# Issuing the value products of two attention pieces as one block, ahead of older work

## The chip, the cores and the metric

The kernel runs on one core of a Trainium2 chip. The metric is device time in microseconds. A time is the median of several runs; the profile shows one further execution. The engines are called as in the profile: PE is TensorE (matmuls), PEld its weight loads, DVE is VectorE, ACT is ScalarE, POOL is GpSimd, and SP issues all DMAs, one after the other, each once its own waits are over.

## The reference

Windowed attention with block summaries, then a mixture of experts on its output, all in float32.

```python
def _attn_ref(q, k, v):                      # 4 batches, 8 heads, 768 positions, 64 wide
    block, window = (32, 16)
    k_sum = k.reshape(B, H, nb, block, D).max(axis=3)
    v_sum = v.reshape(B, H, nb, block, D).mean(axis=3)
    scores_l = scale * np.matmul(q, k.transpose(0, 1, 3, 2))
    mask_l = np.abs(pos[:, None] - pos[None, :]) < window
    scores_s = scale * np.einsum('bhsd,bhnd->bhsn', q, k_sum) + np.log(block)
    scores_all = np.concatenate([np.where(mask_l, scores_l, -1e9), scores_s], axis=-1)
    ...                                      # softmax over the last axis -> a
    return np.matmul(a, np.concatenate([v, v_sum], axis=2))

def _moe_ref(x, domain_probs, w1, w2):       # x is (3072, 512); 4 experts, hidden width 1024
    p = domain_probs / (domain_probs.sum(-1, keepdims=True) + 1e-09)
    for e in range(E):
        out += p[:, e:e + 1] * (np.maximum(x @ w1[e], 0.0) @ w2[e])
```

## The kernel before, in words

**Attention.** The work is cut into 64 pieces: piece n is 96 queries of one batch and four of its eight heads; pieces n - 1 and n (n odd) are the two halves of the heads for the same queries. Batch b has pieces 16b to 16b + 15. A piece runs through `load_piece`, `stage_a` (keys ks, queries qs and values v12, v3 split into a high and a low part on ACT and POOL), `scores` (psc on PE, maxima and row sums on DVE and ACT), `probs` (the probabilities aw, in float16 as a high part, a low part and the block summaries), `transposed` (one DMA on SP turns aw into awT), `values` and `to_x`. `values` is 24 matmuls per piece: for two pairs of heads, six terms of two heads each; a matmul has 64 columns of weights and 96 of output, and the two heads write the lower and the upper 64 partitions. Both pieces of a pair write one PSUM bank, called px with the number of the lower piece, so a block is 48 matmuls. `to_x` brings px to the rows of x. The first eight pieces are handled apart, in `first_tokens`.

**Experts.** x is cut into eight token blocks of 384. Products are done in three terms (high x high, low x high, high x low). For blocks 0 and 1, `plain_units` does the first layer (ph, 128x384 outputs) and `mm2` the second (po, 128x512). Blocks 2 to 7 are done in pairs by `pair_units`, with seven first-layer products in place of eight (banks pha, phb, phc, phd; some of them added up on DVE and ACT between the products). High and low parts of weights are made by ACT and POOL (wh and wl), for some on DVE.

**Batches.** For each batch after the first, `setup_k` loads four chunks of k (kch) and reduces each on DVE to ksr, whose spread copy ks goes out with four DMAs; `setup_v` loads four chunks of v (vch), reduces each to vsr, and `stack_v` scales that on ACT (vs5) and turns it on PE with four transposes (pvs). All these chunks, and the rows that `x_operands` reads back, share two buffers (`CHUNKS = 2`).

**What sets the order.** The text of the program issues attention steps between units of the experts: `steps` gives each step a number, and `advance` issues those whose number has come. The first part, up to piece 8, is kept in program order. From there on (`pinned["rest"] = False`) a scheduler arranges the instructions of every engine: it takes, of those that its own estimate of times holds to be ready, the one with the highest priority, which is the order of the text unless a block is given another. Each engine then runs its own list strictly from front to back, so an instruction that waits holds all behind it.

Of the kernel before, what the change touches and what calls it, by code (L numbers as in the profile page):

```python
# [17 lines left out]
B, H, S, D = 4, 8, 768, 64  # L18
# [14 lines left out]
NEG = -1.0e9 / SCALE  # L33

SHIFT = 1.12
ENDS = (17.52, 25.5, 38.0, 53.0, 68.0, 70.0)
WARM = 11

# [24 lines left out]
def attn_moe(ctx: ExitStack, tc: tile.TileContext, qvL, qv0, v0L, kD, kT, vT, w1L, w2L, dpL, cst, out):  # L63
# [18 lines left out]
    V, A, PL, PE = (Engine(e, "rest") for e in (nc.vector, nc.scalar, nc.gpsimd, nc.tensor))  # L82
    SP = Engine(nc.sync, "load")
# [6 lines left out]
    def spare_x(n):  # L90

        return n % 2 == 1 and n < XFREE
# [29 lines left out]
    def aw_of(n):  # L122
        w = spare_x(n)
        if w not in aw_bufs:
            if w:
                t = sb.tile([QB, 3 * G, P], F16, name="aw1", tag="x", bufs=NX)
            else:
                t = const.tile([QB, 3 * G, P], F16, name="aw0")
            PL.memset(t[:, 2 * G : 3 * G, NST:P], 0.0)
            aw_bufs[w] = t  # L130
        return aw_bufs[w]
# [7 lines left out]
    st = {}  # L139
# [156 lines left out]
    def transposed(n):  # L296
        tag, bufs = ("x", NX) if spare_x(n) else ("awT", 2)
        awT = sb.tile([P, 3 * G, QB], F16, name=f"awT{n}", tag=tag, bufs=bufs)
        SP.dma_start_transpose(out=awT, in_=aw_of(n).rearrange("p a k -> p (a k)"))
        st[n]["awT"] = awT  # L300

    def values(n):
        b, g = n // 16, n % 2
        t = st[n]
        awT, (v12, v3), vs = t["awT"], t["v"], vsum[b]
        if g == 0:
            t["bank"] = ps_av.tile([P, 512], F32, name=f"px{n}", tag="av")
        else:
            t["bank"] = st[n - 1]["bank"]
        px = t["px"] = t["bank"][:, g * 2 * QB : (g + 1) * 2 * QB].rearrange("p (c q) -> p c q", q=QB)  # L310
        for c in range(2):
            terms = []
            for j in (2 * c, 2 * c + 1):
                hi, lo, su = awT[:, j, :], awT[:, G + j, :], awT[:NST, 2 * G + j, :]
                terms.append(
                    (
                        (v12[:, j, 0, :], hi),
                        (v12[:, j, 0, :], lo),
                        (v12[:, j, 1, :], hi),
                        (v12[:, j, 1, :], lo),  # L320
                        (v3[:, j, :], hi),
                        (vs[:, g * G + j, :], su),
                    )
                )
            for m in range(6):
                for o in range(2):
                    PE.matmul(px[o * D : (o + 1) * D, c, :], *terms[o][m], start=m == 0, stop=m == 5)

    def both_values(n):
        values(n - 1)  # L330
        values(n)

    def x_half(name):
        return sb.tile([P, 2, TB], F32R, name=name, tag="x", bufs=NX)
# [581 lines left out]
    for n in range(per, NTB * per):  # L916
        k = n + SHIFT * (n >= 2 * per)
        if n > per + 1:
            steps.append((k - 2.0, load_piece, n))
        steps += [  # L920
            (k - 0.6, stage_a, n),
            (k + 0.0, lambda m: scores(m, 0), n),
            (k + 0.3, lambda m: scores(m, 1), n),
            (k + 0.4, probs, n),
            (k + 0.8, transposed, n),
        ]
        if n % 2:
            steps += [
                (k + (1.5 if n < 2 * per else 2.0), both_values, n),
                (k + (1.8 if n < 2 * per else 2.3), to_x, n),  # L930
            ]
    for b in range(1, B):
        k = 2 * per * b + SHIFT
        steps += [(k - 2.0, setup_k, b), (k - (0.5 if b == 1 else 1.0), setup_v, b)]
# [21 lines left out]
    pos = per  # L956
    for (tbs, experts), end in zip(plan, ENDS):
        pair = tbs if isinstance(tbs, int) else None
        n = 2 if pair else len(tbs)
# [86 lines left out]
```

## Time and profile before

| | |
|---|---|
| median of 3 runs | 1178.43 us (1176.1 to 1181.34) |
| the profiled execution | 1176.52 us |
| its span, first to last instruction | 1174.7 us |
| granted TensorE clock, mean | 0.993 |
| PE busy | 1150.5 us (98%), 7188 matmuls |
| DVE, ACT, POOL busy | 631.4 (54%), 541.2 (46%), 468.5 us (40%) |
| value products px | 1344 matmuls |
| transpositions awT | 56, on SP, median 3.8 us from issue to landing |

Times in the profile's rows are microseconds from the start of the span. A row of the timeline gives start, duration, engine, line of the kernel, operation, out<-in by names (without numbers), the shape, how many equal ones are merged, and in brackets the idle time ahead of it with what ended it. Nearly all instructions are recorded by one helper, so they all have its line; the names tell them apart. TensorE's matmuls overlap, so the distance of two starts tells what one costs, not its duration. The granted clock is the share of full speed at which TensorE was let run.

### The profile page before, as it was taken

Reading aid. Unit: us, or ns where it says so; the run is one execution under the profiler, and the core shown is the slowest. Engines: PE = TensorE matmul, PEld = TensorE weight load, DVE = VectorE, ACT = ScalarE, POOL = GpSimd, SP = SyncE. Lnnn points to the kernel's source line nnn. Section 1 sums busy time; section 2 is a strip of 40 time slices with the busy share of each in tenths; the row PEclk is TensorE's granted clock in tenths of the full one; section 3 lists DMA queues with packets and bytes.
Section 4 is the critical chain, followed back from the end, with each engine's and each line's share of the span. In section 5 each row is a group of like instructions: output and inputs, shape, how many; then the busy total and the mean of one; then the engine's idle time right before and its main releaser. Section 6 shows DMA issues by size and latency. Waiting matters only on the chain.

```text
span 1174.7 us, 20612 instructions
## 1 busy us (share of the span) xinstructions
PE 1150.5 (98%) x7188; PEld 1021.0 (87%) x7188; DVE 631.4 (54%) x1519; ACT 541.2 (46%) x1586; POOL 468.5 (40%) x578
## 2 busy tenths in 40 slices
PE   9898899999979999999999999999999999999998
PEld 7787789998968989898898989889898998989896
DVE  6778775555796837558586543535354222323131
ACT  5678667655666736546375443434343211202020
POOL 2398677846786737547265122221202000000000
PEclk9999999999999999999999999999999999999999
DMA  6699787957996878789963859678571556566531
GB/s 240 227 281 321 225 250 218 305 118 215 307 251 182 272 228 263 225 277 288 320 196 102 255 149 289 202 213 284 141 205 61 159 156 212 165 197 189 163 98 54
DMA packets 202329, 249.66 MB, mean 213 GB/s; under 512 B 82672, under 2 KB 118512, under 8 KB 202224
## 3 DMA queue, kind: packets, MB, share of 16 engines
q1 hardware_dynamic: 202224, 248.34, 69.6%
q8 instruction: 57, 0.93, 0.3%
q14 instruction: 48, 0.39, 0.1%
HBM read 174.22 MB, written 57.15 MB: 197 GB/s over the span
## 4 chain that ended last, share of the span: by engine, by line
PE 85%; DMA 4%; DVE 4%; POOL 3%; ACT 2%; issue 1%; SPq 1%; POOLq 0%; DVEq 0%; ACTq 0%
PE po L75 42%; PE phb L75 13%; PE pha L75 9%; PE ph L75 5%; PE phd L75 4%; PE phc L75 4%; PE psc L75 4%; PE px L75 3%; DMA vch<-in_vT 1%; PE pav L75 1%; DMA wr<-in_w2L 1%; DMA kch<-in_kT 1%; DVE ms L75 1%; SPq L75 1%; ACT ms L75 1%
## 5 line engine op out<-in xcount | busy, mean ns | idle before, releaser
L75 PE MATMUL po<-w,hh 128*128 128x512 f32 x1536 | 480.5, 394 | 0.0
L75 PEld LDWEIGHTS po<-w,hh 128*128 128x128 f32 x1536 | 284.2, 188 | 61.0
L75 PE MATMUL po<-w,hl 128*128 128x512 f32 x768 | 302.8, 397 | 0.0
L75 PEld LDWEIGHTS po<-w,hl 128*128 128x128 f32 x768 | 144.4, 188 | 31.5
L75 POOL TENSOR_TENSOR ks<-kr,ks 128x304 fp32r<-128x304 f32 x112 | 99.7, 897 | 176.8 <-ACT ks L75 160.5
L75 DVE CUSTOM_DVE_ANT_0 ms<-psc,c_sb 96x152 f32<-96x152 f32 x256 | 69.2, 306 | 104.6 <-PE psc L75 103.4
L75 PE MATMUL phb<-xh_t,w1s 128*128 128x384 f32 x384 | 114.2, 338 | 0.1
L75 ACT ACTIVATE ms<-ms,nb 96x152 f32<-96x152 f32 x256 | 104.3, 415 | 16.5 <-DVE nb L75 15.6
L75 PE MATMUL pha<-xh,w 128*128 128x384 f32 x384 | 110.7, 335 | 0.0
L75 DVE SCALAR_TENSOR_TENSOR acc<-po,pw,acc 128x512 f32<-128x512 f32 x72 | 51.9, 746 | 108.8 <-PE po L75 108.8
L75 PE MATMUL ph<-xh,wh 128*128 128x384 f32 x256 | 88.0, 347 | 4.8 <-ACT wh L75 3.7
L75 PE MATMUL ph<-xl,wh 128*128 128x384 f32 x256 | 87.4, 341 | 2.3 <-DVE xl L75 2.3
L75 DVE TENSOR_TENSOR aw<-ms,aw 96x512 f16<-96x512 f32 x112 | 77.2, 723 | 21.5 <-ACT aw L75 21.3
L75 PE MATMUL ph<-xh,wl 128*128 128x384 f32 x256 | 87.1, 341 | 1.2 <-POOL wl L75 1.2
L75 ACT CAST ks<-kr 128x304 fp32r<-128x304 f32 x112 | 48.1, 445 | 80.4 <-PE psc L75 62.9
L75 POOL TENSOR_TENSOR wl<-wr,wh 128x512 fp32r<-128x512 f32 x44 | 62.6, 1425 | 45.0 <-ACT wh L75 44.9
L75 ACT CAST aw<-ms 96x512 f16<-96x512 f32 x112 | 53.3, 523 | 56.3 <-issue 37.8
L75 POOL TENSOR_TENSOR qv<-qv,v 128x256 f32<-128x256 f32 x56 | 40.8, 739 | 78.2 <-ACT v L75 78.0
L75 ACT CAST v<-qv 128x256 bf16<-128x256 f32 x112 | 44.5, 405 | 59.2 <-PE px L75 40.8
L75 PEld LDWEIGHTS phb<-xh_t,w1s 128*128 128x128 f32 x384 | 70.8, 188 | 1.0 <-ACT phb L75 0.2
L75 PEld LDWEIGHTS pha<-xh,w 128*128 128x128 f32 x384 | 70.5, 188 | 0.3
L75 PE MATMUL phb<-xl_t,w1s 128*128 128x384 f32 x192 | 64.3, 335 | 0.0
(122 smaller groups left out, 2169.3 us busy)
## 6 DMA issues: line engine op xcount, KB each, us to landing
w<-wd SPq DMA_DIRECT2D x80, 512.0 KB, 4.4
w1s<-wds SPq DMA_DIRECT2D x112, 256.0 KB, 3.5
w<-wd SPq DMA_DIRECT2D x84, 256.0 KB, 3.4
wr<-in_w1L SPq DMA_DIRECT2D x76, 256.0 KB, 4.3
qv<-in_qvL SPq DMA_DIRECT2D x56, 320.0 KB, 4.4
wd<-w SPq DMA_DIRECT2D x32, 512.0 KB, 4.3
wds<-w1s SPq DMA_DIRECT2D x64, 256.0 KB, 2.7
kr<-in_kD SPq DMA_DIRECT2D x56, 256.0 KB, 3.7
```

The source lines that it names most:

```text
L75: ins = getattr(self.engine, name)(*a, **kw)
```

## The change

`both_values`, which issues the 24 products of piece n - 1 and the 24 of piece n, is put into a block of higher priority: its instructions count as 400 places earlier in the text. And the very first of the 48 products gets a dependency on the transposition of piece n, beside that on piece n - 1 which it had. Nothing else is edited, and the numbers of instructions are the same.

```diff
+AHEAD = 400
...
-        SP.dma_start_transpose(out=awT, in_=aw_of(n).rearrange("p a k -> p (a k)"))
+        st[n]["turned"] = SP.dma_start_transpose(out=awT, in_=aw_of(n).rearrange("p a k -> p (a k)"))
         st[n]["awT"] = awT
...
             for m in range(6):
                 for o in range(2):
-                    PE.matmul(px[o * D : (o + 1) * D, c, :], *terms[o][m], start=m == 0, stop=m == 5)
+                    ins = PE.matmul(px[o * D : (o + 1) * D, c, :], *terms[o][m], start=m == 0, stop=m == 5)
+                    if g == 0 and c == 0 and m == 0 and o == 0:
+                        info = mybir.DependencyInfo(mybir.DependencyClass.Sync, mybir.DependencyReason.DATA)
+                        tc.add_manual_dep(ins.ins, st[n + 1]["turned"].ins.name, info, reason="both pieces")
 
     def both_values(n):
-        values(n - 1)
-        values(n)
+        with tc.high_priority(offset=AHEAD):
+            values(n - 1)
+            values(n)
```

Since the scheduler works by its own estimate of the whole, the edit moves other instructions too. The places below are where it moves what is spoken of later. In the names, the first number is that of the piece or of the batch and part, the last one only tells buffers apart.

TensorE at the block of pieces 44 and 45, before: three of its five parts end or begin in these rows.

```order
L75 MATMUL px44_7811<-awT44_7232,vs2_4141 64x96
L75 MATMUL psc46_1_7689<-ks46_1_7491,qs46_7494 96x152 x4
L75 LDWEIGHTS vs2_4141
L75 MATMUL px44_7811<-awT44_7232,vs2_4141 64x96
L75 MATMUL po2_1_0_7565<-w21_0_7128,hh2_1_0_7124 128x512 x2
L75 MATMUL po2_1_0_7565<-w21_0_7128,hl2_1_0_7125 128x512
```

The scores of piece 46 stand between two products of the same block. In the new order each of the 28 blocks is one run of 48 (in all 57 runs before, 28 now), and this one begins and ends between first-layer products.

TensorE where token block 0 is done and block 1 begins: xh1 and xl1 are its x, which the block px14 completes. Before:

```order
L75 MATMUL px14_1803<-awT15_1779,vs0_689 64x96
L75 MATMUL psc16_0_1918<-ks16_0_1853,qs16_1859 96x152 x3
L75 MATMUL psc16_1_1931<-ks16_1_1856,qs16_1859 96x152 x3
L75 MATMUL ph1_1_4_1940<-xh1_0_1087,wh11_4_1439 128x384
L75 MATMUL ph1_1_5_1980<-xh1_0_1087,wh11_5_1492 128x384
L75 MATMUL ph1_1_6_1999<-xh1_0_1087,wh11_6_1524 128x384
L75 MATMUL ph1_1_7_2032<-xh1_0_1087,wh11_7_1566 128x384
L75 MATMUL ph1_1_4_1940<-xl1_0_1088,wh11_4_1439 128x384
```

Now:

```order
L76 MATMUL px14_1803<-awT15_1779,vs0_689 64x96
L76 MATMUL psc17_0_2019<-ks17_0_1965,qs17_1971 96x152 x4
L76 MATMUL psc17_1_2049<-ks17_1_1968,qs17_1971 96x152 x4
L76 MATMUL pvs1_1883<-c_sb_72,vs5_1_1881 120x128 x4
L76 MATMUL ph1_1_4_1940<-xh1_0_1087,wh11_4_1439 128x384
L76 MATMUL ph1_1_5_1980<-xh1_0_1087,wh11_5_1492 128x384
L76 MATMUL ph1_1_6_1999<-xh1_0_1087,wh11_6_1524 128x384
L76 MATMUL ph1_1_7_2032<-xh1_0_1087,wh11_7_1566 128x384
L76 MATMUL ph1_1_4_1940<-xl1_0_1088,wh11_4_1439 128x384
```

The scores of piece 17 and the four transposes of batch 1 (pvs1), which stood 45 to 93 matmuls behind the block, have come ahead of the first product of block 1. On ACT, likewise, vs5 of batch 1 now stands ahead of the two instructions that make xh1 of pieces 14 and 15; before, these two stood ahead of it.

SP, from the first key chunk of batch 1 to the transposition of piece 14. Before:

```order
L143 DMA kch1_0_1719<-in_kT 128x768
L143 DMA kch1_1_1722<-in_kT 128x768
L75 DMA wd21_7_1673<-w21_7_1670 128x1024
L75 DMA wr11_1_2104<-in_w1L 128x512
L75 DMA_TRANSPOSE awT13_1513<-aw1_887 128x12x96
L143 DMA kch1_2_1725<-in_kT 128x768
L143 DMA kch1_3_1728<-in_kT 128x768
L75 DMA kr17_1790<-in_kD 128x4x128
L75 DMA qv17_1791<-in_qvL 128x640
L75 DMA wr11_2_2129<-in_w1L 128x512
L75 DMA_TRANSPOSE awT14_1691<-aw0_746 128x12x96
```

Now:

```order
L144 DMA kch1_0_1719<-in_kT 128x768
L76 DMA_TRANSPOSE awT13_1513<-aw1_887 128x12x96
L144 DMA kch1_1_1722<-in_kT 128x768
L76 DMA kr17_1790<-in_kD 128x4x128
L76 DMA qv17_1791<-in_qvL 128x640
L144 DMA kch1_2_1725<-in_kT 128x768
L76 DMA wr11_1_2104<-in_w1L 128x512
L76 DMA wr11_2_2129<-in_w1L 128x512
L76 DMA wr11_3_2168<-in_w1L 128x512
L144 DMA kch1_3_1728<-in_kT 128x768
L76 DMA wr10_0_2435<-in_w1L 128x512
L76 DMA_TRANSPOSE awT14_1691<-aw0_746 128x12x96
```

The second and the fourth key chunk have moved behind the transposition of piece 13 and behind three weight loads. After these rows come, now, the first value chunk, the four copies ks1, the second and the third value chunk, a load of weights, the transposition of piece 15 and the fourth value chunk; before, all four value chunks came behind the transposition of piece 15.

## The prediction

> **What bounds the kernel now.** I read the page's busy shares and chain first, then the waits of TensorE, then its timeline.
>
> ```profile
> PE 1150.5 (98%) x7188; PEld 1021.0 (87%) x7188; DVE 631.4 (54%) x1519; ACT 541.2 (46%) x1586; POOL 468.5 (40%) x578
> PE 85%; DMA 4%; DVE 4%; POOL 3%; ACT 2%; issue 1%; SPq 1%; POOLq 0%; DVEq 0%; ACTq 0%
> ```
>
> TensorE is busy 98% of the 1174.7 us span and carries 85% of the chain that ended last. So the end moves only with what TensorE itself does, or waits for. What it waits for, as (sum in us, times, longest):
>
> ```profile
> PE px L75 <- DMA awT<-aw: 9.4, 4, 5.6
> ...
> PE ph L75 <- POOL wl L75: 1.2, 1, 1.2
> ```
>
> The largest wait by far is the one the change touches: a value product (px) for a transposition (awT). The four add up to 9.4 us. The other cost that can move is seen in the timeline of TensorE (start, duration, instruction) at one block of 48 products that already stands together:
>
> ```profile
> 198.99 0.62 PE L75 MATMUL po<-w,hh 128*128 128x512 f32 x2
> 199.45 0.40 PE L75 MATMUL po<-w,hl 128*128 128x512 f32 x1
> 199.78 0.40 PE L75 MATMUL px<-awT,v 128*64 128x96 f16 x10
> ...
> 200.79 0.21 PE L75 MATMUL px<-awT,vs 120*64 120x96 f16 x2
> 200.93 0.57 PE L75 MATMUL psc<-ks,qs 128*96 128x152 f32 x4
> ```
>
> Starts count here, since matmuls overlap. Three po matmuls from 198.99 to 199.45 and on stand 0.23 us apart, but the first px comes 0.33 after a po: 0.10 for entering. The 48 products take 1.15 us (199.78 to 200.93), 0.024 each, of which the last pair spends 0.14 before the next matmul where a pair inside takes about 0.05: 0.09 to 0.10 for leaving. A break inside a block costs both again, **0.20 us**.
>
> **The change part by part, as differences to the profiled execution** (1176.52 us, of which the span is 1174.7; 1.9 us under the median of 1178.43, to which I add the sum at the end).
>
> *Fewer breaks.* In the built program the 28 blocks stand in 57 pieces before and in 28 after: 29 breaks x 0.20 = 5.8 us. Five of them (blocks of pieces 8 to 15) lie ahead of the restart at 134 us treated below, where TensorE is held by others in any case, and count nothing. 24 x 0.20 = **-4.8**. Against it, pieces had filled short waits:
>
> ```profile
> 472.05 0.34 PE L75 MATMUL phb<-xh_t,w 128*128 128x384 f32 x1
> 472.32 0.36 PE L75 MATMUL px<-awT,v 128*64 128x96 f16 x7
> 472.42 0.55 DVE L75 TENSOR_TENSOR phc<-phb,p 128x384 f32<-128x384 f32 x1
> 473.11 0.27 PE L75 MATMUL px<-awT,v 128*64 128x96 f16 x3
> 473.31 0.44 PE L75 MATMUL phb<-xh_t,w1s 128*128 128x384 f32 x1
> ```
>
> Here seven and three px stood while VectorE added phc out of the bank that phb had just finished; without them TensorE waits. Four blocks of the paired stage (pieces 38 to 49) were broken at such places. Bounds: 0 (something else fills), and 4.8 (every break had paid for itself). I take half a microsecond for each of four: **+2.0**.
>
> *Old waits.* Three of the four, and the granted clock (the eighth column, PEclk) in windows that follow such gaps:
>
> ```profile
> 129.82 0.40 PE L75 MATMUL px<-awT,v 128*64 128x96 f16 x10 [1.14 <-DMA awT<-aw]
> 332.90 0.40 PE L75 MATMUL px<-awT,v 128*64 128x96 f16 x10 [1.32 <-DMA awT<-aw]
> 349.95 0.61 PE L75 MATMUL px<-awT,v 128*64 128x96 f16 x10 [5.55 <-DMA awT<-aw]
> ...
> 135.00:139.00 4.00, 4.00 (x16) 4.00 (x15) 2.89 (x6) 2.22 (x6) 3.14 (x4) 0.57 1.06 359
> 333.00:336.00 3.00, 3.00 (x37) 2.56 (x37) 3.00 (x5) 1.65 (x5) 2.92 (x4) 1.00 0.95 259
> 350.00:354.00 4.00, 4.00 (x34) 3.46 (x34) 2.36 (x5) 3.04 (x10) 1.82 (x4) 0.52 0.96 286
> ```
>
> The fourth (the rest of the 9.4, 1.4 us at 92) gains nothing: ten microseconds later TensorE waits for POOL's wl (1.2, above), which does not come earlier. That at 129.82 is replaced by the restart below. At 349.95 both halves now stand behind 17 po and 8 psc that used to come after: 17 x 0.23 + 8 x 0.085 = 4.6 us of work inside the wait of 5.55, less 0.3 for the first half, which is now paid behind the landing: -4.3. At 332.90 the block also moves back and gains 0.6. Together **-4.9**, bounds -9.4 (nothing waits) and -3.
>
> *A restart that comes late.* At 134 us token block 0 is done and TensorE starts on block 1, which needs x from pieces 14 and 15. In the new order of TensorE the four transposes pvs1 stand ahead of that restart, and they need all four value chunks of batch 1. On SP the second key chunk has slipped behind the transposition of piece 13.
>
> ```profile
> 107.29 0.92 SPq L143 DMA_DIRECT2D kch<-in_kT  x2
> ...
> 112.08 1.69 SPq L75 DMA_TRANSPOSE awT<-aw  x1
> ...
> 121.89 2.61 SPq L75 DMA_DIRECT2D ks<-ksr  x4
> 126.44 1.31 SPq L75 DMA_TRANSPOSE awT<-aw  x1
> 127.80 1.30 SPq L143 DMA_DIRECT2D vch<-in_vT  x2
> ...
> kch<-in_kT SPq DMA_DIRECT2D x12, 384.0 KB, 5.4
> vch<-in_vT SPq DMA_DIRECT2D x12, 384.0 KB, 5.0
> ...
> L75 DVE TENSOR_REDUCE vsr<-vch x12: 936/952/955, 132.0 to 574.7; 128x24 f32<-128x768 f32 x12
> ...
> 145.39 0.61 ACT L75 ACTIVATE vs<-vsr 128x480 f32<-128x480 f32 x1
> ...
> 134.24 0.44 PE L75 MATMUL ph<-xl,wh 128*128 128x384 f32 x1 [2.30 <-DVE xl L75]
> ```
>
> Chunks share two buffers, so each load waits for a reduction: 5.4 or 5.0 to land (the two rows' last number) plus 0.95. Along the second buffer: SP is free of awT13 at 112.08 + 1.69 = 113.8; kch1_1 reduced at 120.1; kch1_3 at 126.5; four ks issues (2.6) stand ahead of vch1_1: 129.1, reduced at 135.0; vch1_3 at 141.0; vs5 on ScalarE 0.6: 141.6. Behind vs5 on ScalarE now stand the xh of pieces 14 and 15, and on VectorE their xl: about 1.5 more, so TensorE restarts at 143.1 instead of 134.24. Of the 8.9 us it gets back 1.2 (scores 17 and pvs1, done already). With the fastest landings near it (4.2 each, 127.80 to the reduction's start at 132.0) the same sum gives 138.9: +3.5. The other end is that pvs1 comes no earlier than before, when vs5 ended at 146.0 and the restart would fall at 147.5: +12. I take **+6**, nearer the walked orders.
>
> *New waits.* A block's first product now waits for the second transposition, and all of TensorE behind it. The rows give issue, landing (a row's last number) and where the block stood:
>
> ```profile
> 171.68 2.29 SPq L75 DMA_TRANSPOSE awT<-aw  x1
> DMA to landing us min/median/max: 5.7/5.7/5.7
> 175.77 0.23 PE L75 MATMUL px<-awT,v 128*64 128x96 f16 x1
> ...
> 236.57 1.65 SPq L75 DMA_TRANSPOSE awT<-aw  x1
> DMA to landing us min/median/max: 3.8/3.8/3.8
> 246.36 0.40 PE L75 MATMUL px<-awT,v 128*64 128x96 f16 x10
> ...
> 469.52 1.74 SPq L75 DMA_TRANSPOSE awT<-aw  x1
> DMA to landing us min/median/max: 4.7/4.7/4.7
> ```
>
> Block 18 stands where its single first product stood (175.77) and its second transposition lands at 177.4: 1.6. Block 24 moves ahead of 50 ph (0.173 each) and 4 psc, 9.0 us: it comes at 237.4, its transposition at 240.4, less 1.0 since SP issues it before a load that it used to follow: 2.0. Block 40 stands at 472.3 to 472.6, landing 474.2: 1.5. Blocks 16, 20, 22, 26 and 48 meet their landings within half a microsecond by the same comparison, counted at nothing; the twelve others of the later stages have 2 us or more to spare. **+5**, bounds 1 (ScalarE and VectorE deliver earlier) and 9.
>
> The window rows above weigh one more thing: a wait of 1.32 leaves the clock at 1.00, gaps of 2.30 and 5.55 halve it for some 4 us, 1.7 to 1.9 us each. The old halvings at 135 and 350 are about replaced by one behind the later restart, and new waits of 1.5 to 2.0 lie between the rows; I count no difference. The Trainium skill, in "TensorE: Matmul & The Clock Gate", Part 1, has the throttle return after an idle window of about 3.4 us. By that rule the 2.30 us gap would have cost nothing and new waits under 3.4 us could not halve the clock; the row of 135 to 139 us (0.57) says otherwise, so the measurement decides, and the sum by the rule would be some 2 us lower.
>
> *Covered.* ScalarE's casts of v wait for a px four pieces earlier; where a first half now comes later they wait longer. The cover is that TensorE hardly waits for them at any place beside the restart; were it gone, it would show as a wait of psc for ks.
>
> **Sum:** -4.8 + 2.0 - 4.9 + 6 + 5 = +3.3 us. On the profiled execution 1179.8; on the median 1181.7, so **1182**.
>
> **Rivals.**
> 1. *Slower: pvs1 holds the restart to the old time of vs5.* For it: every chunk's reduction, and ScalarE, stand in queues that wait for the same loads. Against it: three of four value loads are issued earlier. Restart +12 instead of +6: +9.3, **1188**. It decides once vs5 ends after about 143.
> 2. *Slower: each new wait halves the clock.* For it, 0.57 after 2.30; against it, 1.00 after 1.32. Three times 1.7: +8.4, **1187**.
> 3. *Faster: the restart keeps its time,* because the loads land early or the schedule upstream runs ahead, and the transpositions are ready: 0 for the restart, +1 for new waits: -6.7, **1172**. Against it: the order puts pvs1, and ScalarE's xh, behind the last chunk.
> That the blocks do not stand together is excluded by the order.
>
> **How the numbers follow.** A measurement of this kernel tells about 0.5%, 6 us, from no change (its three runs lie 5.2 apart). Forecast 0.45; rival 1 0.28; rival 2 0.12; rival 3 0.15. The first is no change, the next two slower, the last faster. Its own range is 1176 to 1186; the range takes in rival 3 at 1172, and rivals 1 and 2 with both upper bounds partly met, 1193. Beyond it on both sides I leave 2 in 10.
>
> **What would show it.** Each px row of the timeline counts 48 in a run. The first pvs starts near 140 (before 149.7) and the first ph<-xl behind it near 141 to 143, with ScalarE's vs or VectorE's xl as releaser of a wait of 4 us or more. Waits of px for awT: about 5 us at 176, 238 and 473, and 1 to 2 at 350. I am wrong if the restart is at 136 or earlier, or if waits for awT stay under 3 us or pass 10.

## The result, and the profile after

The change makes the kernel slower: 1185.07 us (median of 6 runs, 1180.37 to 1187.83) beside 1177.17 of the kernel before on the same chip, a ratio of 1.006 with a 95% interval of 1.0034 to 1.0085, or +4 to +10 us. The profiled execution took 1185.61 us, its span 1183.7 against 1174.7. The numbers of lines are one higher (L76 for L75, L144 for L143), since the change adds a constant.

Busy shares and the chain, from the page of the changed kernel:

```profile
PE 1149.8 (97%) x7188; PEld 1023.8 (86%) x7188; DVE 623.0 (53%) x1519; ACT 543.3 (46%) x1586; POOL 465.1 (39%) x578
PE 78%; DMA 5%; POOL 2%; ACT 2%; DVE 1%; issue 1%; SPq 0%; POOLq 0%; ACTq 0%
```

TensorE's busy time is 0.7 us lower, so it did not get more work: it waits more. What it waits for after (sum in us, times, longest):

```profile
PE px L76 <- DMA awT<-aw: 8.2, 5, 3.2
PE ph L76 <- ACT wh L76: 5.2, 4, 2.4
PE psc L76 <- DVE acc L76: 4.9, 1, 4.9
PE psc L76 <- POOL qs L76: 2.6, 2, 2.4
PE psc L76 <- DVE nb L76: 1.5, 1, 1.5
```

The products' waits for transpositions are hardly less, 8.2 in place of 9.4, and scores (psc) now wait 1.5 us or more in three places, where before none waited over 0.6. Two places hold most of these waits. The first is the restart at token block 1, in TensorE's timeline:

```profile
133.33 2.47 PE L76 MATMUL psc<-ks,qs 128*96 128x152 f32 x8 [4.87 <-DVE acc L76]
138.57 0.61 PE L76 MATMUL px<-awT,v 128*64 128x96 f16 x10 [2.77 <-DMA awT<-aw]
...
140.64 1.56 PE L76 MATMUL psc<-ks,qs 128*96 128x152 f32 x8
143.11 1.11 PE L76 MATMUL pvs<-c_sb,vs 128*120 128x128 f32 x4 [0.91 <-ACT vs L76]
...
145.30 0.52 PE L76 MATMUL ph<-xl,wh 128*128 128x384 f32 x1
```

The block of 48 products stands in a run from 138.57 to 140.64. The first ph<-xl comes at 145.30; before, it came at 134.24. The wait of 4.87 is put down to DVE's acc, but the load of the scores' weights (PEld) at the same moment waits for ScalarE's cast of ks, which waits for POOL's kr, which waits for the spread ks1 of the key maxima. The timelines of PEld, POOL and ScalarE there:

```profile
133.33 0.58 PEld L76 LDWEIGHTS psc<-ks,qs 128*96 128x96 f32 x2 [5.30 <-ACT ks L76]
...
132.54 0.47 POOL L76 COPY kr<-ks 128x96 f32<-128x96 f32 x2 [1.13 <-DMA ks<-ksr]
...
132.84 1.48 ACT L76 CAST ks<-kr 128x304 fp32r<-128x304 f32 x4 [1.55 <-POOL kr L76]
...
142.46 0.60 ACT L76 ACTIVATE vs<-vsr 128x480 f32<-128x480 f32 x1
...
143.26 0.54 ACT L76 ACTIVATE xh<-px 128x192 fp32r<-128x192 f32 x2
```

And SP's queue ahead of it, with two of the four key chunks (the first and the last), the spread ks1 (x4) and the transpositions of pieces 13 and 15:

```profile
112.94 0.42 SPq L144 DMA_DIRECT2D kch<-in_kT  x1
114.18 2.27 SPq L76 DMA_TRANSPOSE awT<-aw  x1
...
121.48 0.33 SPq L144 DMA_DIRECT2D kch<-in_kT  x1
...
127.83 2.62 SPq L76 DMA_DIRECT2D ks<-ksr  x4
...
132.70 1.59 SPq L76 DMA_TRANSPOSE awT<-aw  x1
```

The key chunks of batch 1 begin to go out at 112.94 (before: 107.29), and the spread at 127.83 (121.89), 5.65 and 5.94 us later. On DVE the third reduction waits 1.00 for its chunk and holds the maxima of piece 15's second half (124.66) behind it. The last reduction (126.85) holds little: rs, behind it, still waits 0.19 for ScalarE. So awT15 goes out at 132.70 (126.44):

```profile
123.79 0.95 DVE L76 TENSOR_REDUCE ksr<-kch 128x24 f32<-128x768 f32 x1 [1.00 <-DMA kch<-in_kT]
124.66 0.30 DVE L76 CUSTOM_DVE_ANT_0 ms<-psc,c_sb 96x152 f32<-96x152 f32 x1
...
126.85 0.95 DVE L76 TENSOR_REDUCE ksr<-kch 128x24 f32<-128x768 f32 x1 [0.28 <-DMA kch<-in_kT]
127.99 0.30 DVE L76 TENSOR_SCALAR rs<-rs 96x4 f32<-96x4 f32 x1 [0.19 <-ACT ms L76]
...
131.70 0.94 DVE L76 TENSOR_TENSOR aw<-ms,aw 96x512 f16<-96x512 f32 x2
```

The transposition then also lands more slowly: the trace gives awT15 5.8 us from issue to landing, 3.3 before. These 2.5 us are most of px14's wait of 2.77, and no run here tells what makes the landing slow.

The second place is where the old wait of 5.55 us stood (349.95). It is gone from there, and two others have come:

```profile
355.84 0.57 PE L76 MATMUL psc<-ks,qs 128*96 128x152 f32 x4 [2.40 <-POOL qs L76]
...
362.09 0.61 PE L76 MATMUL px<-awT,v 128*64 128x96 f16 x10 [3.21 <-DMA awT<-aw]
```

**Where the 9 us of the span came from.** One and the same matmul can be found in both traces. The difference of its two starts, less the work that the new order has put ahead of it, is what the kernel has lost or gained up to there. This is worked out from the starts of all matmuls, at the stage bounds given in times of the kernel before; the last column is the difference at the last matmul, in us. (The spans can differ by up to 1.2 us more, since the end behind the last matmul takes 4.1 to 5.3 us: from48's span is 3.1 shorter than before, not 4.3.) A stage in which nothing is edited differs by up to 1.4 us (right behind a late restart, in only14 and upto13, by 2.4 and 2.6), the one at 110 to 145 by up to 2.1, so less than that is not read; behind 365 us unedited stages agree within 0.3.

| kernel | to 110 | 110-145 | 145-300 | 300-365 | 365-460 | 460-510 | 510-640 | from 640 | sum |
|---|---|---|---|---|---|---|---|---|---|
| whole change | 1.7 | **7.2** | -1.2 | **1.3** | -1.1 | **3.4** | 0.1 | **-2.4** | 9.0 |
| pieces 16 to 63 (from16) | 0.0 | -0.1 | 1.3 | 0.4 | -1.5 | 1.7 | 0.0 | -2.4 | -0.5 |
| pieces 8 to 15 (upto15) | 4.9 | 5.3 | -1.4 | 0.0 | 0.0 | 0.0 | 0.0 | 0.2 | 9.1 |
| dependency alone (dep_only) | 0.4 | 6.4 | -0.1 | -0.6 | 0.0 | -0.1 | 2.5 | 0.0 | 8.5 |
| priority alone (prio_only) | 5.6 | 4.6 | 2.7 | 1.3 | -1.2 | 2.3 | -1.3 | -1.4 | 12.6 |
| pieces 8 to 13 (upto13) | 1.6 | 5.0 | 2.6 | 0.6 | 0.0 | 0.0 | 0.0 | 0.0 | 9.8 |
| pieces 14, 15 (only14) | 3.5 | 1.8 | 2.4 | 0.0 | 0.0 | 0.0 | 0.0 | 0.0 | 7.7 |
| whole change, early keys (keys_early) | 2.6 | 0.1 | 2.2 | 2.3 | -1.4 | 2.2 | 0.0 | -2.4 | 5.7 |
| before, early keys (keys_early_b) | 4.3 | 1.0 | 0.6 | -1.4 | 0.0 | 0.0 | 0.1 | 0.0 | 4.7 |
| pieces 48 to 63 (from48) | 0.1 | -1.2 | -0.4 | 0.0 | 0.0 | 0.0 | -0.4 | -2.4 | -4.3 |
| pieces 36 to 39, 48 to 63 (best) | 5.4 | -0.6 | -0.9 | -0.4 | -1.4 | 1.5 | -0.4 | -2.4 | 0.8 |
| pieces 16 to 63 but 30, 31 (no30) | 3.6 | -0.4 | 3.6 | 0.5 | -1.3 | 1.9 | 0.0 | -2.4 | 5.5 |
| pieces 48 to 63, two aw (f48_x34) | 2.2 | -2.1 | 0.4 | -2.3 | 0.0 | 0.0 | -0.4 | -2.4 | -4.6 |

The first column matters for reading all others: up to 75 us every engine runs the same instructions in every one of these kernels, and from16, from48, only14, no30, best and f48_x34 keep the order of before until behind 110 us; yet their single executions come there 0 to 5.4 us late. So a span carries up to 5 us that belong to no edit, and the verdicts below go by the ratios of many runs, while the table tells the place.

### The profile page after: what moved, and what is told of

It is laid out like the page before. It is cut to its first block, busy times and chain, and to the rows that moved or that the text cites. A ratio compares the mean times of both kernels' runs of the same rounds, so it can differ in the third digit from the quotient of the medians.

```text
span 1183.7 us, 20625 instructions
## 1 busy us (share of the span) xinstructions
PE 1149.8 (97%) x7188; PEld 1023.8 (86%) x7188; DVE 623.0 (53%) x1519; ACT 543.3 (46%) x1586; POOL 465.1 (39%) x578
## 4 chain that ended last, share of the span: by engine, by line
PE 78%; DMA 5%; POOL 2%; ACT 2%; DVE 1%; issue 1%; SPq 0%; POOLq 0%; ACTq 0%
PE po L76 41%; PE phb L76 12%; PE pha L76 8%; PE ph L76 6%; PE phd L76 4%; PE phc L76 4%; PE psc L76 2%; PE px L76 2%; DMA wr<-in_w1L 2%; DMA awT<-aw 1%; POOL wr L76 1%; POOL ks L76 1%; DMA qv<-in_qvL 1%; DMA kr<-in_kD 1%; POOL qs L76 0%
## 5 line engine op out<-in xcount | busy, mean ns | idle before, releaser
L76 PE MATMUL po<-w,hh 128*128 128x512 f32 x1536 | 480.5, 394 | 0.0
L76 PEld LDWEIGHTS po<-w,hh 128*128 128x128 f32 x1536 | 286.4, 189 | 61.5
L76 PE MATMUL po<-w,hl 128*128 128x512 f32 x768 | 302.9, 398 | 0.0
L76 POOL TENSOR_TENSOR ks<-kr,ks 128x304 fp32r<-128x304 f32 x112 | 98.3, 885 | 215.3 <-ACT ks L76 192.4
L76 PEld LDWEIGHTS po<-w,hl 128*128 128x128 f32 x768 | 144.7, 189 | 31.4
L76 DVE CUSTOM_DVE_ANT_0 ms<-psc,c_sb 96x152 f32<-96x152 f32 x256 | 69.2, 306 | 106.2 <-PE psc L76 102.3
L76 ACT ACTIVATE ms<-ms,nb 96x152 f32<-96x152 f32 x256 | 104.3, 415 | 34.1 <-DVE nb L76 33.4
L76 PE MATMUL phb<-xh_t,w1s 128*128 128x384 f32 x384 | 115.3, 340 | 1.1 <-ACT phb L76 0.9
L76 DVE SCALAR_TENSOR_TENSOR acc<-po,pw,acc 128x512 f32<-128x512 f32 x72 | 52.2, 746 | 114.8 <-PE po L76 114.8
L76 PE MATMUL pha<-xh,w 128*128 128x384 f32 x384 | 110.9, 336 | 0.0
L76 ACT CAST ks<-kr 128x304 fp32r<-128x304 f32 x112 | 48.1, 444 | 108.9 <-PE psc L76 93.7
L76 PE MATMUL ph<-xh,wh 128*128 128x384 f32 x256 | 87.9, 347 | 6.4 <-ACT wh L76 5.2
L76 PE MATMUL ph<-xh,wl 128*128 128x384 f32 x256 | 86.2, 337 | 0.5 <-POOL wl L76 0.4
L76 PE MATMUL ph<-xl,wh 128*128 128x384 f32 x256 | 86.5, 338 | 0.0
L76 POOL TENSOR_TENSOR wl<-wr,wh 128x512 fp32r<-128x512 f32 x44 | 61.9, 1412 | 52.3 <-ACT wh L76 43.0
L76 DVE TENSOR_TENSOR aw<-ms,aw 96x512 f16<-96x512 f32 x112 | 72.7, 683 | 16.7 <-ACT aw L76 15.9
L76 ACT CAST aw<-ms 96x512 f16<-96x512 f32 x112 | 53.4, 524 | 59.8 <-issue 40.9
L76 PEld LDWEIGHTS phb<-xh_t,w1s 128*128 128x128 f32 x384 | 71.4, 189 | 2.9 <-ACT phb L76 1.5
L76 PEld LDWEIGHTS psc<-ks,qs 128*96 128x96 f32 x448 | 55.1, 167 | 20.1 <-ACT ks L76 5.5
L76 PEld LDWEIGHTS pha<-xh,w 128*128 128x128 f32 x384 | 71.0, 189 | 0.3
L76 PE MATMUL psc<-ks,qs 128*96 128x152 f32 x448 | 57.5, 252 | 10.6 <-DVE acc L76 4.9
L76 PE MATMUL phb<-xl_t,w1s 128*128 128x384 f32 x192 | 64.7, 337 | 0.0
```

The costliest lines, as they stand in the source:

```text
L76: ins = getattr(self.engine, name)(*a, **kw)
```

## The experiments

In the selections below only the blocks named are treated as the change does (both the priority and the dependency); the rest stand as before. Times are medians, the ratios are to the runs of before on the same chip, with 95% intervals.

**Which blocks lose: pieces 16 to 63 (from16), 8 to 15 (upto15), 48 to 63 (from48).**

```diff
-        with tc.high_priority(offset=AHEAD):
+        with ExitStack() as rush:
+            if n >= 2 * per:              # upto15: n < 2 * per; from48: n >= 48
+                rush.enter_context(tc.high_priority(offset=AHEAD))
             values(n - 1)
             values(n)
...
-                    if g == 0 and c == 0 and m == 0 and o == 0:
+                    if g == 0 and c == 0 and m == 0 and o == 0 and n >= 2 * per:
```

from16: 

> The change for the blocks of pieces 16 to 63 only; the four blocks of pieces 8 to 15, ahead of the restart at token block 1, are treated as before. Theory A (the restart is the loss: in the two traces, with the work done by each instruction's place taken off, the distance between the kernels grows by 7.2 us between 110 and 145 us and by about 0 from there to the end): the first ph<-xl is back at 133 to 136 us and the time is 1176 to 1179, no more than 1 us from before. Rival B (the waits for the second transposition at the later blocks, and the stalls at 353 and 358 us that took the place of the old 5.55, are the loss; the late restart of the profiled run was inherited from its first 70 us, which ran 2.6 us late in an unchanged order): the time stays at 1183 to 1186.

upto15: 

> The change for the four blocks of pieces 8 to 15 only; everything behind is treated as before. Theory A: the restart is late again, first ph<-xl at 143 to 146 us, and the time is before + 6 to 8, 1183 to 1186. Rival B: first ph<-xl at 134 to 139 us, time before + 0 to 3.

from48: 

> The change for the blocks of pieces 48 to 63 only: eight blocks, 17 pieces in place of 8 in the built order's last stages, and no wait above 0.35 us at them in the trace of the changed kernel. Theory A (a break costs 0.20 us): before - 1.8 to - 2.7 us (that stage of the changed kernel gained 2.7), time 1174.5 to 1176. Rival C (the breaks filled short waits, so closing them brings nothing; the 2.7 came from elsewhere): before - 0.5 to + 0.5.

Measured: from16 1177.88 us, ratio 1.0000 (0.9985 to 1.0015); upto15 1183.77, 1.0052 (1.0034 to 1.0071); from48 1174.93, 0.9977 (0.9963 to 0.9991); before 1177.78. Theory A stands in all three times; upto15's restart came at 146.42, 0.4 behind A's bound, in an execution that was 4.9 late at 110 us already. In TensorE's timeline of from16 the restart is back where it was, and the stall at 350 is there:

```profile
134.14 0.44 PE L76 MATMUL ph<-xl,wh 128*128 128x384 f32 x1 [2.17 <-DVE xl L76]
...
348.68 0.57 PE L76 MATMUL psc<-ks,qs 128*96 128x152 f32 x4 [2.43 <-POOL qs L76]
...
354.70 0.61 PE L76 MATMUL px<-awT,v 128*64 128x96 f16 x10 [2.97 <-DMA awT<-aw]
```

So the four blocks of pieces 8 to 15 carry nearly all of the loss, by the ratios 6 of 7 us, and the 24 others come out at zero: by the table, what the late stages gain, the middle ones give back.

**Which half of the change: the dependency alone (dep_only), the priority alone (prio_only).** In effect:

```diff
-        with tc.high_priority(offset=AHEAD):      # dep_only: without it
-            values(n - 1)
-            values(n)
+        values(n - 1)
+        values(n)
...
-                        tc.add_manual_dep(...)    # prio_only: without it
```

dep_only: 

> The dependency of a block's first product on the second transposition for every block, without the raised priority. Its order is that of the changed kernel until after the restart, and behind it 46 pieces stand in place of 28. Theory A: the restart as late as with the whole change (143 to 146 us), time before + 6 to 9, 1183 to 1186: the dependency alone, not the priority, brings the loss. Rival D (the raised priority puts the transposes pvs1 and the blocks ahead of older work, and that is the loss): restart at 134 to 137 us, before + 0 to 2.

prio_only: 

> The raised priority for every block, without the dependency: a block's first half goes as soon as its own transposition is there, and 45 pieces stand in place of 28 (57 before). If the dependency is what makes the restart late (its half alone cost 7.5 us): restart at 133 to 138 us, no wait of px18, px24 or px40 for a second transposition over 0.5 us, and the time within 2 us of before, 1175 to 1179. If the priority is as harmful (it pulls blocks ahead of po and psc, whose late results DVE and ScalarE then pass on): before + 4 or more, 1181 or later.

Measured: dep_only 1185.28 us, 1.0070 (1.0046 to 1.0094; before 1177.78); prio_only 1188.82, 1.0091 (1.0061 to 1.012; before 1176.35). With the dependency alone the restart came at 143.16, and restart and time are as theory A said. Its "not the priority" fell: of the two cases set out for the priority alone the second came, and it costs at least as much as the whole. What both have in common shows in the scores ahead of the restart, in dep_only's timeline of TensorE:

```profile
130.85 2.46 PE L76 MATMUL psc<-ks,qs 128*96 128x152 f32 x8 [3.63 <-ACT ks L76]
```

And in that of prio_only:

```profile
137.36 0.79 PE L76 MATMUL psc<-ks,qs 128*96 128x152 f32 x2 [3.68 <-ACT ks L76]
```

Here the wait is named for what it is: ks16, the end of the chain from the key chunks. In dep_only and in the whole change the chunks are late since SP issues them behind a later piece; in prio_only SP has four weight loads ahead of awT13 and the last two key chunks. Any disturbance of the pieces ahead of the restart seems to end at this chain.

**Which path into the restart: pieces 8 to 13 (upto13), 14 and 15 (only14).**

```diff
+    def together(n):
+        return n < 15                     # only14: n == 15
...
-        with tc.high_priority(offset=AHEAD):
+        with ExitStack() as rush:
+            if together(n):
+                rush.enter_context(tc.high_priority(offset=AHEAD))
...
```

upto13: 

> The change for the blocks of pieces 8 to 13 only, so without the last block ahead of the restart. On SP the order is that of the changed kernel until behind the last key chunk and awT15; on TensorE the first half of px14 stands ahead of psc16 again and pvs1 behind the restart, and on ScalarE xh of pieces 14 and 15 ahead of vs5. Two parts of the late restart are told apart. A1 (the key chunks of batch 1 come late, since they are issued behind a later qv16 and awT13: psc16 waited until 133.3 us, and awT15 behind it until 138.5): psc16 starts at 131 to 134 us again. A2 (vs5 and pvs1 stand ahead of xh: vs5 ended at 143.06 and xh ran at 143.26, though px14 was done at 140.7): gone here, worth 2.5 for ScalarE and 1.6 for pvs1 and its wait, less the pvs1 that is done later, 3.5 in all. Both together: restart at 140 to 142 us, before + 2 to 3.5 us, 1180 to 1181.5. If A1 alone carried the loss, before + 5 to 7; if A2 alone, restart at 134 to 137 and before + 0 to 1.

only14: 

> The change for the block of pieces 14 and 15 alone. SP keeps the order of before until behind the restart, and pvs1 stays behind it. Theory A (the loss comes from what the earlier blocks, 8 to 13, do to the loads): the restart stays at 133 to 136 us and the time within 1 us of before, 1177 to 1179. Rival: the wait of both halves of px14 for awT15, right ahead of the restart, is itself the loss: restart at 137 or later, before + 3 or more.

Measured: upto13 1182.85 us, 1.0051 (1.0033 to 1.0069); only14 1180.78, 1.0022 (1.0008 to 1.0036); before 1177.34. TensorE's timeline of upto13:

```profile
132.73 2.47 PE L76 MATMUL psc<-ks,qs 128*96 128x152 f32 x8 [3.71 <-DVE acc L76]
139.56 0.61 PE L76 MATMUL px<-awT,v 128*64 128x96 f16 x10 [4.37 <-DMA awT<-aw]
...
143.26 0.33 PE L76 MATMUL ph<-xl,wh 128*128 128x384 f32 x1
...
162.90 0.73 PE L76 MATMUL po<-w,hh 128*128 128x512 f32 x2 [2.17 <-DVE hl L76]
```

vs5 and pvs1 no longer stand ahead of xh here, and nothing is won by it (upto15: 1.0052): the second half of px14 waits for awT15 until 139.56, and what pvs1 had filled comes back as a wait of 2.17 for hl. So A1 is enough for this loss, and A2 adds nothing that shows in the time. In only14 the key chunks keep their place, but both halves of px14 wait right ahead of the restart:

```profile
134.62 0.61 PE L76 MATMUL px<-awT,v 128*64 128x96 f16 x10 [3.65 <-DMA awT<-aw]
...
139.47 0.69 PE L76 MATMUL ph<-xl,wh 128*128 128x384 f32 x1 [0.17 <-DVE xl L76]
```

That costs 2.6 us (0.9 to 4.2), more than the 1 us that theory A allowed and near the 3 of the rival. The restart at 139.47 is 136.0 less the 3.5 by which this execution was late at 110 us, at A's upper bound. So holding the first half back seems a loss of its own. That it does not add to that of the earlier blocks, since there psc16 waits first, is argued, not shown.

**The key chunks asked for one piece earlier: with the whole change (keys_early), and alone (keys_early_b).**

```diff
-        steps += [(k - 2.0, setup_k, b), (k - (0.5 if b == 1 else 1.0), setup_v, b)]
+        steps += [(k - (2.0 if b > 1 else 3.0), setup_k, b), (k - (0.5 if b == 1 else 1.0), setup_v, b)]
```

keys_early: 

> The whole change, with the key chunks of batch 1 asked for one piece earlier, so that on SP the last key chunk stands right behind awT12, the ks1 spread ahead of awT14 and awT15 ahead of the last two value chunks. Theory A1 (the lateness of the key chunks, and of what DVE and SP hold behind them, is the late restart): psc16 starts without a wait of 3 us, awT15 lands at 128 to 133 us, the restart is at 134 to 138 us, and 4 to 6 us of the whole change's loss of 7.5 come back: before + 1 to 3.5, 1178 to 1181. Rival G (the blocks of pieces 8 to 13, which wait for their second transposition, hold everything back themselves, whenever the chunks are loaded): restart at 140 us or later, before + 5 or more.

keys_early_b: 

> The kernel before, with the key chunks of batch 1 asked for one piece earlier and nothing else: the control of the run above. If the earlier chunks are worth something by themselves, the restart comes ahead of 134.2 us and the time falls by as much. Theory A1 expects little, since here psc16 did not wait for them (0.4 us): between before - 1.5 and before + 1.5.

Measured: keys_early 1182.85 us, 1.0055 (1.0036 to 1.0074); keys_early_b 1180.19, 1.0025 (1.0013 to 1.0037); before 1177.03. SP's queue in keys_early, with the last key chunk and the spread:

```profile
107.86 0.91 SPq L144 DMA_DIRECT2D kch<-in_kT  x1
...
116.04 2.60 SPq L76 DMA_DIRECT2D ks<-ksr  x4
```

TensorE's timeline of keys_early:

```profile
131.67 0.40 PE L76 MATMUL px<-awT,v 128*64 128x96 f16 x10 [1.27 <-DMA awT<-aw]
...
137.91 0.69 PE L76 MATMUL ph<-xl,wh 128*128 128x384 f32 x1 [1.04 <-DVE xl L76]
...
180.95 0.40 PE L76 MATMUL px<-awT,v 128*64 128x96 f16 x10 [1.31 <-DMA awT<-aw]
```

The restart comes back from 145.30 to 137.91, and the stage from 110 to 145 costs 0.1 in place of 7.2: by these traces the key chunks are the cause there, as A1 says. But the time hardly follows: it is 5.8 us over before, where A1 gave 1 to 3.5 and rival G 5 or more. The earlier chunks cost 2.9 us by themselves (the control was expected at no more than 1.5), and blocks behind the restart wait (1.31 at 180.95, for awT19). Against its control the whole change costs 3.5 us here, with the interval 1 to 6, against 7.1 (4 to 10) without the early chunks: the same direction, with intervals that overlap. That a restart on time would leave the change without a loss is not shown.

**Why the old wait of 5.55 came back: without the block of pieces 30 and 31 (no30), and with a second aw buffer (f48_x34).**

```diff
+    def together(n):
+        return n > 16 and n != 31         # no30, with the rest as in upto13
...
-XFREE = 28
+XFREE = 34                                # f48_x34, which is from48 with this line
```

no30: 

> The change for the blocks of pieces 16 to 63 without that of pieces 30 and 31. In the trace with 16 to 63, px32 waits until 354.65 for awT33, 4.7 us later than before, and psc35 waits 2.6 us. Theory E (the first half of px30, held back to the landing of awT31, gives its awT buffer back 12 us later, at 334.5 in place of 322.2; awT32 is issued at 341.05 in place of 336.05, and awT33, whose aw buffer waits for awT32, lands 4.7 later): with px30 in two halves again awT33 lands at 349 to 351 us, the wait of px32 falls under 1.5 us, and the time is 3 to 4 us under that of 16 to 63: 1174 to 1175. Rival F (awT33 is late for the order on SP or the wait of psc35 for qs35, whatever px30 does): awT33 lands at 353 us or later, and the time stays at 1177 to 1178.

f48_x34: 

> The change for the blocks of pieces 48 to 63 only, with the odd pieces 29, 31 and 33 given a second aw buffer as the odd pieces before them have (XFREE 34 for 28). Theory H (from piece 28 on there is one aw buffer, so aw33 is written only once awT32 has landed, 340.16, and awT33 lands 9.7 us behind it, wherever TensorE's products stand: that is why the wait of 5.55 came back as 2.57 and 3.36): awT33 lands at 341 to 346 us and the wait of px32 falls under 1 us; time 3 to 5 us under from48, before - 5 to - 8, 1170 to 1172.5. Rival I (POOL's and ScalarE's work for pieces 34 and 35 is as late, so another wait takes the place): a wait of psc35 or px32 of 2 us or more stays, time within 1.5 us of from48.

Measured: no30 1177.02 us, 1.0004 (0.999 to 1.0018; before 1177.34); f48_x34 1172.37, 0.996 (0.9946 to 0.9975; before 1177.03). In no30 psc35 and px32 wait as long as in from16, in an execution that is 7.2 us later at this place by the stage table's reckoning:

```profile
355.24 0.57 PE L76 MATMUL psc<-ks,qs 128*96 128x152 f32 x4 [2.48 <-POOL qs L76]
...
359.05 0.61 PE L76 MATMUL px<-awT,v 128*64 128x96 f16 x10 [2.96 <-DMA awT<-aw]
```

awT32 is indeed issued early again (344.03 less 7.2), yet awT33 is not (355.46 less 7.2, 348.3, near the 348.92 of from16), so theory E explains only the first step, and F is right about the time. Nor is it the aw buffer there: awT32 lands 3.4 us after its issue, at 347.4, and ScalarE writes aw33 only at 349.33. The constant XFREE moves not only aw, but also awT and ks of pieces 29, 31 and 33 to other buffers. With it awT33 goes out early; SP's queue in f48_x34:

```profile
337.55 1.67 SPq L76 DMA_TRANSPOSE awT<-aw  x1
```

On TensorE px32 then does not wait at all; what waits there now are three scores, of pieces 34, 35 and 36:

```profile
334.58 0.57 PE L76 MATMUL psc<-ks,qs 128*96 128x152 f32 x4 [1.79 <-POOL qs L76]
...
348.64 0.57 PE L76 MATMUL psc<-ks,qs 128*96 128x152 f32 x4 [1.34 <-POOL qs L76]
...
363.72 0.57 PE L76 MATMUL psc<-ks,qs 128*96 128x152 f32 x4 [1.64 <-POOL qs L76]
```

So the buffers of these pieces make awT33 late. That it is the one of aw (H) is not shown apart from those of awT and ks; in the changed kernel, though, ScalarE's write of aw33 at 352.16 waits for awT32, which lands then. Behind it stand POOL's and ScalarE's parts for the next pieces (I): the three scores wait 4.8 us where px30 and px32 had waited 6.9. The stage gains 2.3 us in this trace. By the time both theories fall just short: 4.7 us under before where H gave 5 to 8, and 2 under from48 where I gave at most 1.5. This is the fastest version here, by 0.4% against before (0.25 to 0.54); its interval overlaps that of from48, and no run has the buffers without the change, so what they are worth alone is open.

**A selection by the table (best).** The blocks whose stages gain, with `together(n)` as `n in (37, 39) or n >= 49`.

best: 

> The change for the blocks of pieces 36 to 39 and 48 to 63 only: those whose stages gained in the traces (1.5 us between 365 and 460 us, 2.8 behind 598) and that showed no wait of 0.45 us or more at a block or a score. Expected: before - 3.5 to - 4.5 us, 1173 to 1174.5. If the breaks are worth 0.20 us each (14 fewer): before - 2.8.

Measured: 1177.20 us, 0.9995 (0.998 to 1.001; before 1177.34). The gain expected did not show. Its table row has -1.4 from 365 to 460, and then +1.5 behind it, where px40 and the scores beside it wait 0.2 to 0.6 us each for results of DVE: the gain of pieces 36 to 39 is handed back at the next block. Behind 510 us it gains the same 2.8 as from48. That from48's time shows these 2.8 and best's does not lies where the two intervals overlap, and no run here settles it.

## Why the prediction was off, by its own steps

Forecast +3.3, measured +7.1 (4 to 10) by the ratio; 1185.07 lies inside the range, 3 us above the likeliest, and on the side of rivals 1 and 2, slower by more than 0.5%. For the pieces 16 to 63 the terms gave -4.8 + 2.0 - 4.9 + 5 = -2.7, and from16 measured 0.0 (-1.8 to 1.8). For the restart they gave +6, and upto15 measured +6.1 (4.0 to 8.4).

- **Old waits, -4.9: the step that failed.** The stage from 300 to 365 us shows no gain: +1.3 (0.4 in from16), no more than an unedited stage differs. I moved TensorE's block back and let awT33 land at its old time. But the transposition moves as well: awT33 goes out at 356.07 in place of 345.00, 11.1 us later, in a kernel that is 8 to 9 us late there, and lands in 6.0 us in place of 4.9. ScalarE and POOL are no earlier with pieces 34 and 35. f48_x34 shows what helped: more buffers upstream, not another place on TensorE.
- **Fewer breaks, -4.8.** The price was too low, not too high. From 598 us, where its blocks wait for nothing, from48 gains 2.8 us for ten breaks, 0.28 each in place of 0.20, and the stage from 640 gives -2.4 in every kernel in which its blocks are whole. 365 to 460 gives -1.1 to -1.5 for five breaks (four in best).
- **Fillers lost, +2.0, and px40's wait, 1.5.** From 460 to 640 the stages gave +3.5 (from16: +1.7) although seven breaks went there, worth 2.0 at 0.28 each: a cost of 5.5 (3.7) where these two terms had 3.5. The place was right, the form was not: px40 itself finds its transposition there, and a score ahead of it waits 1.5 for nb (the last row of the waits), where pieces of px had stood.
- **New waits at px18 and px24, 3.6.** px18 does not wait; px24 does, 0.7 in the whole change and 1.9 in from16.
- **Late restart, +6.** Right in size, partly by luck: the walk itself came to 8.9 less 1.2, I took a little less, and the path was one short of the cause. The walk along SP and the chunks is what happened, but not through vs5: the restart was held by ks16, which hangs on the key chunks, and by awT15, which hangs on them in part and landed slowly, and upto13 shows that without vs5 and pvs1 ahead of xh it costs the same. The forecast named the key chunk that slips behind awT13 and then followed only what this does to the value chunks.
- **No clock difference.** The windows of the changed kernel around its restart (PEclk is the eighth column) say otherwise:

```profile
130.00:135.00 5.00, 1.54 (x5) 1.02 (x5) 4.81 (x8) 2.44 (x6) 3.52 (x7) 0.73 0.72 199
135.00:140.00 5.00, 2.20 (x40) 1.98 (x41) 3.07 (x13) 2.52 (x11) 3.02 (x5) 0.50 1.12 297
140.00:145.00 5.00, 4.09 (x34) 3.76 (x31) 3.37 (x13) 3.96 (x13) 3.38 (x6) 0.50 0.47 156
```

  Busy time at these clocks, 0.27 x 1.5 + 0.5 x (2.2 + 4.1) = 3.6 us, against 1.7 for the one halving before. (The 0.73 includes idle time at full clock; with 0.5 throughout it is 3.9.) By this estimate some 2 of the 7.2 us there are clock.
- **Rivals.** Rival 1 had the point from which it decides right (vs5 ended at 143.06), but upto13 refutes its mechanism. Rival 2 gets the two us of clock at the restart, not at the new waits it named: no wait at px18 or px40, and px24's is 0.7. Rival 3 fell with the restart.
- **What would show it.** The blocks stand 48 in a run; pvs1 (143.1) and ph<-xl (145.3) came 2 to 3 us later than forecast, but not behind the wait of 4 us or more that I named: pvs1 waits 0.91 for vs, and ph<-xl not at all. Waits for awT add up to 8.2, but mainly at 139 and 362 us, not at 176, 238 and 473.

## What to carry to other kernels

A wait at one engine for a transfer is a place in a ring: before moving the waiter, follow the buffer that the transfer needs, and ask whether the landing moves with it. A block ordered to wait for its last input holds back what the earlier inputs would have released, and here the price was paid at the next place where TensorE had nothing else to do, through the chain of the key chunks; the priority alone cost as much. Closing a break gained time where nothing waited, and lost some where the pieces had filled a wait, so such an order is better tried stage by stage.

## What was not expected of the hardware

**Runs of the same instructions part early.** best has the order of before on all engines until behind 320 us; its first key chunk goes out at 109.98, against 107.29 in the prediction's row:

```profile
109.98 0.92 SPq L144 DMA_DIRECT2D kch<-in_kT  x2
```

**The length of a wait does not tell whether the clock halves.** Windows of the changed kernel behind its waits of 2.40, 3.21 and 1.46 us:

```profile
355.80:358.40 2.60, 2.56 (x16) 2.23 (x17) 2.53 (x5) 0.51 (x3) 2.54 (x5) 1.00 1.00 326
362.00:366.00 4.00, 3.91 (x52) 3.44 (x53) 4.00 (x13) 4.00 (x15) 2.56 (x3) 0.50 0.49 166
480.00:484.00 4.00, 3.65 (x14) 3.65 (x15) 2.74 (x13) 4.00 (x16) 3.92 (x6) 0.57 1.10 243
```

The one of 2.40 leaves it at 1.00, the one of 1.46 halves it, and the prediction's bound between 1.32 and 2.30 does not hold. In from16 the same score waits 1.49, and the clock stays:

```profile
472.50:476.50 4.00, 4.00 (x65) 3.68 (x66) 2.92 (x11) 4.00 (x17) 3.92 (x5) 1.00 1.13 279
```

The Trainium skill's idle window of about 3.4 us ("TensorE: Matmul & The Clock Gate", Part 1) would excuse the 2.40 but not the 1.46, so the rows decide against it as a rule for single gaps; what does decide, no run here shows.
